# A fused pooled-attention, Fourier-mixing and two-layer channel block: the third batch's front end in the second block, later stages moved by one to three groups, and the residual in three tiles

## The chip, the cores and the metric

The kernel runs on one core of one Trainium2 chip. A core has five engines with queues of their own: TensorE (PE, and PEld for its weight loads), VectorE (DVE), ScalarE (ACT), GpSimd (POOL) and SyncE (SP, which issues most DMAs). The metric is the device time of one execution in microseconds; a lower time is better. A program is timed several times and the median counts; besides, one execution is recorded by the hardware profiler, and its trace is what is read here.

## The reference

Eight batches of eight heads, 576 tokens, 64 channels a head, go through an attention whose keys and values are means over eight neighbouring tokens (72 keys). The result, as 512 channels for each token, is mixed by a two-dimensional Fourier transform, normalised over the channels, and put through two layers with a relu between:

```
k_p = k.reshape(B, H, 72, 8, D).mean(axis=3)       # B, H, S, D = 8, 8, 576, 64
v_p = v.reshape(B, H, 72, 8, D).mean(axis=3)
attn = softmax(scale * q @ k_p^T)
x = (attn @ v_p) as [B, S, 512]
u = x + real(fft(fft(x, axis=1), axis=2))
un = (u - mean(u)) / sqrt(var(u) + 1e-6)           # over the 512 channels
out = u + relu(un @ w_ch1) @ w_ch2                 # 512 -> 2048 -> 512
```

All is float32. The matmuls of the two layers split each operand in a high part and a rest, and add three products (high x high, high x rest, rest x high).

## The kernel before

**Two streams of work.** The first is the *front end* of a batch, function `fe(b)` (L313): everything from the load of q and k to the normalised operands `unh{b}` and `unl{b}`. It is a generator of 31 steps; each `yield` ends one. The second is the *main loop*, `fast()` (L863) with `plain()` (L840) for its first block: the two layers over nine blocks of 512 tokens. As a batch has 576 tokens, block k takes the first tokens of batch k and what was left of batch k-1, so block k cannot begin before the front end of batch k has written its operands, and the second product group of a block reads the last of them.

**The front end's steps,** with the names used below (the digit behind a name is the batch): load of q and k, and the sums of eight keys on POOL (L344, tile `ks`); the scores `psS` on PE (L409), their maxima on DVE (L411, L414) and exponentials on ACT (L418); the transposes `psT`, `psV` and `psR` (L446, L456, L467); the products with v, `psX` (L489); a split of the result in a high part and a residue `f` (L573, L574); the first Fourier side `psA` (L613) and `psB` (L630); the second, `psQ` and `psP` (L647), whose sums go through DVE (L653 to L663) and POOL (L674 to L682) into `U` or `X`; the mean over channels `psM` (L719, L723); the centred tokens (L725); their squares `lf` on ACT and DVE (L734 to L740); the variance `psVar` on PE: L749 to L754 from batch 2 on, where ACT casts half of the squares (`qhl`, L749) and DVE the rest (L750), and L767 to L786 with diagonal tiles `dg` for batches 0 and 1; three Newton rounds on ACT and DVE for one over the root (L755 to L762); the scaling on POOL (L794); the operands (L701 to L705).

**The main loop's steps.** In block 0, `plain()` runs a group of twelve matmuls (tile `g`, L850) for each of 16 rows of channels, then the relu and its residue (L855, L856), and then `gemm2` (L814) adds the row's part of the second layer into `acc`, twelve matmuls in three pieces of four. From block 1 on, a step takes two rows of channels at once: seven product groups of six matmuls (`x`, L911), whose sums run through DVE (L870 and L915), and two relus (L878 to L880), with the pieces of the second layer of the step before ("g" in the lists `MID`, `FIRST`, `LAST`) between them. All PSUM banks but `acc`'s are shared from then on: products and front-end tiles take the next of four buffers of one tag in turn (`shared`, L293). At a block's end `evict` (L825) adds `acc` to the residual `U` and sends it out (L838).

**What sets the order.** The main loop counts its groups: `pos` in the listing. At each group `advance(pos)` (L965) takes a front-end step of batch c when `pos` has passed the entry of a table for that step plus the batch's start, `90 + 104 * (c - 2)`, or 0 for batch 1. So an entry is the number of groups from the start of the block ahead of the batch's own; a negative entry lies in the block before that. Batch 1 has the table `AT1`, batch 2 `AT2`, all others `AT` (L57 to L59). Up to group 92 (`MANUAL`) the order on PE is the scheduler's, which may move an instruction; behind it PE runs in program order. The order on the other engines is the scheduler's throughout. An engine runs its queue in order: what waits holds up all behind it.

**The residual and the staged weights.** `U` (L121) is one tile, `[128, 4, 1728]`, with three slots of 576 columns, and batch b lives in slot `b % 3` (`slot`, L75). Ahead of the main loop its first two slots hold q and k of batch 0, and the third takes pieces of the weights as they come from memory: `load_w` (L166) brings each piece to one of four places, two in that third slot and two in `sx`; `prep_w` (L184) then splits it with ACT, DVE and POOL operations (L194 to L208), `combine` (L223) makes sums of pieces (L235), and DMAs write them to scratch memory, from where `feed` (L258) brings them back block by block through a ring of twelve buffers.

Of the kernel before, what the change touches and what calls it, by code (L numbers as in the profile page):

```python
# [22 lines left out]
P = 128  # L23
# [51 lines left out]
def slot(b):  # L75
    return (b % 3) * S


def cuts(t0, t1, every):

    r = []
    while t0 < t1:
        e = min(t1, (t0 // every + 1) * every)
        r.append((t0, e))
        t0 = e
    return r

# [6 lines left out]
def tile_kernel(ctx: ExitStack, tc: tile.TileContext, qt, kt, vm, vr, w1, w2, cad, cbd, mkd, out):  # L94
    nc = tc.nc
    cp = ctx.enter_context(tc.tile_pool(name="cp", bufs=1))
# [34 lines left out]
    def flat(t):  # L131
        return t.rearrange("p c n -> p (c n)")
# [33 lines left out]
    def load_w(n):  # L166
# [928 lines left out]
```

## Time and profile before

| | |
|---|---|
| median of three runs | 1133.4 us (1131.36, 1133.4, 1134.22) |
| the profiled execution's own time | 1137.14 us |
| its span, first to last instruction | 1135.3 us |
| mean granted tensor clock over the span | 0.954 |
| end of block 0's stretch, first product of block 1 | 267.15 us |
| first products of blocks 2 to 6 | 386.15, 502.37, 617.39, 733.5, 850.4 us |
| memory traffic | 217.63 MB read, 30.67 MB written |

A row of the timeline has a start in microseconds, the duration, the engine, the line, the operation, `out<-in` by the program's names without their numbers, the tiles' sizes and the number of instructions taken together; in brackets stands how long the engine idled ahead of the row, and the instruction that ended the wait. A granted clock of 1.00 is full speed. The profiled execution is one execution of its own, a little longer than the median of the runs.

### The profile page before, as it was taken

What the parts mean: (1) busy time and instruction counts of PE and PEld (TensorE: products, weight loads), DVE (VectorE), ACT (ScalarE), POOL (GpSimd) and SP (SyncE); (2) the same over time, 40 slices, a digit from 0 to 9 for tenths busy, and PEclk for the clock granted to TensorE, in tenths of its full rate; (3) what the DMA queues carried; (4) which work ended last, traced back from release to release, by engine and by line L of the source; (5) the groups of instructions that cost most, each with busy time, mean ns of one, the idle gap of its engine ahead of it and who ended that gap; (6) DMA issues with size and microseconds to landing.
All of it is one profiled execution on the core that took longest, in us unless ns stands there. A gap on an engine that the chain in (4) does not pass through costs nothing.

```text
span 1135.3 us, 19340 instructions
## 1 busy us (share of the span) xinstructions
PE 1028.5 (91%) x6118; PEld 887.8 (78%) x6118; DVE 754.9 (66%) x1479; ACT 568.0 (50%) x1698; POOL 574.1 (51%) x531
## 2 busy tenths in 40 slices
PE   6778988767899899999999999999999999999998
PEld 4456666546788788888888888888888988988987
DVE  7579865877767775777578766876687567433333
ACT  6577754555435653576346734574367333322221
POOL 4357566663663656465645564556554244322221
PEclk8789988987999999999999999999999999999999
DMA  8628858454666676677766776777576667888884
GB/s 284 201 74 269 305 164 274 147 191 158 225 212 208 185 262 216 195 214 254 234 190 218 246 249 187 220 247 239 187 216 194 202 199 225 287 262 255 294 258 144
DMA packets 142756, 249.58 MB, mean 220 GB/s; under 512 B 15808, under 2 KB 36288, under 8 KB 142400
## 3 DMA queue, kind: packets, MB, share of 16 engines
q1 hardware_dynamic: 142368, 245.69, 67.7%
q0 software_dynamic: 288, 2.66, 0.6%
q8 instruction: 50, 0.82, 0.3%
q14 instruction: 50, 0.41, 0.1%
HBM read 217.63 MB, written 30.67 MB: 219 GB/s over the span
## 4 chain that ended last, share of the span: by engine, by line
PE 53%; DVE 17%; ACT 11%; DMA 7%; issue 5%; POOL 4%; SPq 0%; DVEq 0%; POOLq 0%; ACTq 0%
PE acc L814 24%; PE x L911 20%; ACT t L418 2%; PE psS L409 2%; DMA sx<-in_w 2%; DMA k<-in_kt 2%; PE psP L647 1%; PE psB L630 1%; DMA w1op<-w1s 1%; DMA out<-U 1%; DVE sx L870 1%; PE psX L489 1%; DVE lf L740 1%; DVE X L705 1%; PE psQ L647 1%
## 5 line engine op out<-in xcount | busy, mean ns | idle before, releaser
L911 PE MATMUL x<-unh,w1op 128*128 128x256 f32 x1792 | 345.4, 282 | 17.1 <-DVE R L475 3.7
L911 PEld LDWEIGHTS x<-unh,w1op 128*128 128x128 f32 x1792 | 289.3, 189 | 53.5 <-DVE sx L870 6.0
L870 DVE TENSOR_TENSOR sx<-x,sx 128x256 f32<-128x256 f32 (+1 forms) x384 | 176.1, 464 | 144.7 <-PE x L911 137.2
L880 POOL TENSOR_TENSOR hl<-sx,hh 128x512 fp32r<-128x512 f32 x128 | 171.3, 1338 | 199.7 <-ACT hh L879 179.8
L878 ACT ACTIVATE sx<-sx 128x512 f32<-128x512 f32 x128 | 80.9, 632 | 218.4 <-DVE sx L870 218.1
L911 PE MATMUL x<-unl,w1op 128*128 128x256 f32 x896 | 176.7, 279 | 0.0
L814 PE MATMUL acc<-hh,w2low 128*128 128x512 f32 x576 | 167.4, 405 | 0.0
L911 PEld LDWEIGHTS x<-unl,w1op 128*128 128x128 f32 x896 | 136.9, 189 | 0.0
L814 PEld LDWEIGHTS acc<-hh,w2low 128*128 128x128 f32 x576 | 102.1, 192 | 15.2
L814 PE MATMUL acc<-hh,w2high 128*128 128x512 f32 x324 | 94.1, 398 | 5.0 <-ACT hh L855 5.0
L418 ACT ACTIVATE t<-psS,mx 128x72 f32<-128x72 f32 x280 | 86.4, 345 | 21.0 <-DVE mx L414 12.5
L814 PE MATMUL acc<-hl,w2high 128*128 128x512 f32 x324 | 93.7, 397 | 0.0
L426 POOL TENSOR_TENSOR t<-t,sm 128x720 f32<-128x720 f32 x32 | 47.7, 1492 | 76.1 <-DVE sm L425 52.3
L879 ACT CAST hh<-sx 128x512 fp32r<-128x512 f32 x128 | 79.4, 620 | 3.7
L814 PE MATMUL acc<-hl,w2h 128*128 128x512 f32 x252 | 75.9, 425 | 1.5 <-DVE hl L856 1.5
L814 PE MATMUL acc<-hh,w2h 128*128 128x512 f32 x252 | 71.2, 406 | 4.0 <-ACT hh L855 4.0
L814 PEld LDWEIGHTS acc<-hh,w2high 128*128 128x128 f32 x324 | 56.4, 190 | 13.7 <-ACT hh L855 5.7
L409 PE MATMUL psS<-kpb,q 128*128 128x144 f32 x280 | 51.3, 336 | 14.6 <-DVE R L475 7.2
L418 ACT ACTIVATION_READ_ACCUMULATOR t<-psS,mx 128x1 f32 x280 | 64.4, 231 | 0.0
L814 PEld LDWEIGHTS acc<-hl,w2high 128*128 128x128 f32 x324 | 56.6, 189 | 8.5 <-issue 0.4
L409 PEld LDWEIGHTS psS<-kpb,q 128*128 128x128 f32 x280 | 46.6, 229 | 19.4 <-DVE R L475 7.8
L344 POOL TENSOR_TENSOR k<-k 128x288 f32<-128x288 f32 (+1 forms) x56 | 36.1, 645 | 48.9 <-DMA k<-in_kt 47.5
(267 smaller groups left out, 1959.3 us busy)
## 6 DMA issues: line engine op xcount, KB each, us to landing
w1op<-w1s SPq DMA_DIRECT2D x448, 256.0 KB, 3.4
w2low<-w2l SPq DMA_DIRECT2D x128, 256.0 KB, 3.4
w2high<-w2d SPq DMA_DIRECT2D x72, 256.0 KB, 3.7
U<-in_w SPq DMA_DIRECT2D x16, 512.0 KB, 4.5
sx<-in_w SPq DMA_DIRECT2D x16, 512.0 KB, 5.1
q<-in_qt SPq DMA_DIRECT2D x28, 288.0 KB, 3.0
k<-in_kt SPq DMA_DIRECT2D x28, 288.0 KB, 2.9
v<-in_vm SPq DMA_DIRECT2D x28, 256.0 KB, 2.8
```

Source lines behind the costliest of these rows:

```text
L344: nc.gpsimd.tensor_tensor(out=out if n == 1 else src[:, :, 0:n], in0=src[:, :, 0] if n == 1 else src[:, :, 0:n], in1=src[:, :, 1] if n == ...
L409: nc.tensor.matmul(ps[:, c * W2J:(c + 1) * W2J], lhsT=q[:, r0:r0 + P], rhs=kpb[g % 2], start=True, stop=True)
L418: nc.scalar.activation(t[:, c0 + c, h], pv[:, c, h], AF.Exp, scale=1.0 / 64.0, bias=mx[x], accum_out=sm[x])
L426: ins = nc.gpsimd.tensor_tensor(out=t, in0=t, in1=sm.unsqueeze(3).broadcast_to([P, 5, 2, J]), op=ALU.mult)
L489: behind["X", b] = nc.tensor.matmul(ps, lhsT=w, rhs=a, start=(i == 0), stop=(i == len(mm) - 1))
L647: nc.tensor.matmul(ps, lhsT=w, rhs=a, start=(i == 0), stop=(i == 6))
L814: nc.tensor.matmul(acc[e], lhsT=a[:, e], rhs=h, start=(f == 0 and x == 0), stop=(f == NFC - 1 and x == 2))
L870: nc.vector.tensor_tensor(out=o, in0=x, in1=y, op=ALU.add)
L878: nc.scalar.activation(c, c, AF.Relu)
L879: nc.scalar.copy(out=h, in_=c)
L880: nc.gpsimd.tensor_tensor(out=l, in0=c, in1=raw(h), op=ALU.subtract)
L911: nc.tensor.matmul(ps, lhsT=w[:, q, i], rhs=t[:, 2 * c + i], start=(n == 0), stop=(n == 5))
```

## The change

The table of batch 2 is rewritten: its first entry was -36, in block 0, and is now -6 with the next at 3, and its last ones before 104, from 76 to 79, are now 88 to 90. In the table of batches 3 to 7, `AT`, thirteen entries grow by one or two groups and two shrink by one; the variance's (index 25, `psVar`) goes from 76 to 78. The tile `U` becomes three tiles `Us[0]` to `Us[2]`, and the two places for staged weights in the third of them become contiguous pieces of 1024 columns. The functions `slot` and `cuts` (which nothing calls) go. The set of instructions is the same before and after.

```
@@ -26,7 +26,6 @@
-RING = 3 * S
@@ -54,8 +53,8 @@
 RES = [0, 2, 5, 7, 9, 12, 14]
 
 UNITS0, UNITS, MANUAL, TAIL = 90, 104, 92, (2, 8, 14, 20, 26)
-AT = [-36, -28, -23, -5, -3, -1, 2, 13, 14, 16, 18, 25, 27, 28, 38, 41, 44, 47, 51, 52, 55, 57, 60, 66, 66, 76, 76, 77, 78, 79, 104]
-AT2 = [-36, -28, -23, -13, -11, -9, -6] + AT[7:]
+AT = [-36, -28, -23, -5, -2, 0, 3, 13, 14, 16, 19, 25, 27, 28, 39, 42, 45, 48, 51, 52, 55, 57, 60, 65, 65, 78, 78, 79, 80, 81, 104]
+AT2 = [-6, 3, 7, 20, 23, 25, 28, 30, 32, 38, 41, 46, 48, 48, 58, 60, 63, 65, 67, 67, 70, 72, 74, 78, 78, 88, 88, 89, 89, 90, 104]
 AT1 = [-1] * 7 + [2 + 3.5 * n for n in range(17)] + [64, 69, 71, 73, 74, 75, 96]
 E0, O0, E1, O1 = 0, 1, 2, 3
 
@@ -70,20 +69,6 @@
-def slot(b):
-    return (b % 3) * S
...
@@ -118,7 +103,7 @@
     rw = [cp.tile([96, P], F32R, name=f"rw{i}") for i in range(2)]
     xe = cp.tile([P, 290], F32R, name="xe")
     X = cp.tile([P, 4, S], F32, name="X")
-    U = cp.tile([P, 4, RING], F32, name="U")
+    Us = [cp.tile([P, 4, S], F32, name=f"U{i}") for i in range(3)]
     rb = cp.tile([P, S + 1024], F32, name="rb")
     xt0 = rb[:, 2 * S:2 * S + 256].rearrange("p (c n) -> p c n", c=4)
     uns = {}
@@ -172,7 +157,7 @@
             return
         x = place[n]
         if x < 2:
-            st = U[:, 2 * x:2 * x + 2, 2 * S:2 * S + DM].bitcast(I32)
+            st = flat(Us[2])[:, 1024 * x:1024 * (x + 1)].bitcast(I32).rearrange("p (r x) -> p r x", r=2)
         else:
             st = sx[:, 1024 * (x - 2):1024 * (x - 1)].bitcast(I32).rearrange("p (r x) -> p r x", r=2)
         nc.sync.dma_start(st, src.bitcast(I32).rearrange("p (r x) -> p r x", r=2))
@@ -311,17 +296,16 @@
 
 
     def fe(b):
-        ro = slot(b)
-        Ub = U[:, :, ro:ro + S]
+        Ub = Us[b % 3]
         Xb = Ub if b else X
         st = {}
         halves = [slice(0, HS), slice(HS, S)]
 
         def load(g):
 
-            k = U[:, g, S:2 * S] if b == 0 else wk.tile([P, S], F32, tag="k", name=f"k{b}_{g}")
+            k = Us[1][:, g] if b == 0 else wk.tile([P, S], F32, tag="k", name=f"k{b}_{g}")
             nc.sync.dma_start(k, kt[b, g])
-            q = U[:, g, 0:S] if b == 0 else wk.tile([P, S], F32, tag="q", bufs=2, name=f"q{b}_{g}")
+            q = Us[0][:, g] if b == 0 else wk.tile([P, S], F32, tag="q", bufs=2, name=f"q{b}_{g}")
             nc.sync.dma_start(q, qt[b, g])
             st["q", g], st["k", g] = q, k.rearrange("p (j w) -> p j w", w=POOLW)
 
@@ -828,7 +812,7 @@
             for b, t0, n, col in segs:
                 if n == 0:
                     continue
-                y = slice(slot(b) + t0, slot(b) + t0 + 2 * n)
+                U, y = Us[b % 3], slice(t0, t0 + 2 * n)
                 a = acc[e].rearrange("p (h x) -> p h x", h=2)[:, :, col:col + n]
                 u = U[:, e, y].rearrange("p (h x) -> p h x", h=2)
                 if k == 0:
```

What the tables do to the queues is shown by the order of the instructions, before and after. A row is one instruction, or as many alike as the x at its end tells; the names carry numbers here, the first of which is the batch (`psS2_3_0` is a score tile of batch 2).

The first place is TensorE around the first product of block 1, `x<-unh1`. Before, the rows ahead of it are:

```order
L785 MATMUL psVar1_1968<-dg_2001,avg_75 128x288
L446 MATMUL psT2_2_2080<-ident_74,t2_2_1866 128x128 x4
L785 MATMUL psVar1_1968<-dg_2001,avg_75 128x288
L456 MATMUL psV2_0_2097<-ident_74,t2_3_1769 128x128
L456 MATMUL psV2_0_2097<-ident_74,t2_2_1866 128x128
L457 MATMUL psV2_0_2097<-ident_74,rt_1796 32x128
L467 MATMUL psR2_0_2105<-ident_74,rt_1796 32x128 x4
L409 MATMUL psS2_0_0_2128<-kpb0_76,q2_0_1919 128x144 x3
L409 MATMUL psS2_0_3_2140<-kpb0_76,q2_0_1919 128x144 x2
L409 MATMUL psS2_1_0_2175<-kpb1_77,q2_1_1929 128x144 x3
L409 MATMUL psS2_1_3_2187<-kpb1_77,q2_1_1929 128x144 x2
L911 MATMUL x_2251<-unh1_2017,w1op_2054 128x256 x2
```

After the change the same place reads:

```order
L631 MATMUL psP1_2_1616<-cb_72,A0_1287 128x290 x3
L631 MATMUL psP1_2_1616<-cb_72,A1_1288 128x290 x3
L631 MATMUL psP1_2_1616<-cb_72,AB2_1289 128x290
L703 MATMUL psM1_1704<-s_1656,avg_75 128x288
L703 MATMUL psM1_1707<-s_1656,avg_75 128x288
L751 MATMUL psVar1_1821<-avg_75,lf_1756 128x1 x5
L769 MATMUL psVar1_1821<-dg_1854,avg_75 128x288 x2
L895 MATMUL x_2033<-unh1_1870,w1op_1907 128x256 x2
L895 MATMUL x_2033<-unl1_1871,w1op_1907 128x256 x2
L895 MATMUL x_2033<-unh1_1870,w1op_1907 128x256 x2
L393 MATMUL psS2_3_0_2044<-kpb1_77,q2_3_1960 128x144 x3
L393 MATMUL psS2_3_3_2056<-kpb1_77,q2_3_1960 128x144 x2
```

Batch 2's scores and transposes have left the stretch between batch 1's last stages and block 1; its first scores stand behind block 1's first product group. From batch 1's `psB` to its `psVar` no row of another kind stands between.

The second place is TensorE in the last third of block 3, where batch 4's variance is computed. Before:

```order
L911 MATMUL x_6185<-unh3_3696,w1op_6084 128x256 x2
L911 MATMUL x_6185<-unl3_3697,w1op_6084 128x256 x2
L911 MATMUL x_6185<-unh3_3696,w1op_6084 128x256 x2
L753 MATMUL psVar4_6201<-qhl_6198,avg_75 128x288
L754 MATMUL psVar4_6201<-qhl_6198,avg_75 128x288
L753 MATMUL psVar4_6205<-qhl_6198,avg_75 128x288
L754 MATMUL psVar4_6205<-qhl_6198,avg_75 128x288
L409 MATMUL psS5_3_0_6217<-kpb1_77,q5_3_6108 128x144 x3
L409 MATMUL psS5_3_3_6229<-kpb1_77,q5_3_6108 128x144 x2
L814 MATMUL acc3_0_5335<-hl_6043,w2h_69 128x512
```

After:

```order
L393 MATMUL psS5_3_3_6215<-kpb1_77,q5_3_6110 128x144 x2
L798 MATMUL acc3_0_5337<-hl_6045,w2h_69 128x512
L798 MATMUL acc3_1_5338<-hl_6045,w2h_69 128x512
L798 MATMUL acc3_2_5339<-hl_6045,w2h_69 128x512
L798 MATMUL acc3_3_5340<-hl_6045,w2h_69 128x512
L895 MATMUL x_6260<-unh3_3669,w1op_6088 128x256 x2
L895 MATMUL x_6260<-unl3_3670,w1op_6088 128x256 x2
L895 MATMUL x_6260<-unh3_3669,w1op_6088 128x256 x2
L737 MATMUL psVar4_6271<-qhl_6268,avg_75 128x288
L738 MATMUL psVar4_6271<-qhl_6268,avg_75 128x288
L737 MATMUL psVar4_6275<-qhl_6268,avg_75 128x288
L738 MATMUL psVar4_6275<-qhl_6268,avg_75 128x288
```

The variance of batch 4 now stands behind batch 5's scores, a piece of the second layer and one more product group; before, it stood ahead of those scores.

The third place is POOL in block 0, at the residue `f` of batch 1 that `psB` reads. Before (`wdh` are sums of weights, `ks` sums of keys, `v2` and `k2` tiles of batch 2):

```order
L235 TENSOR_TENSOR wdh_86<-wdh_86,wdl_87 128x512
L344 TENSOR_TENSOR ks_1658<-k2_3_1650 128x72
L208 TENSOR_TENSOR w2low_1504<-wdl_87,w2high_1502 128x512
L235 TENSOR_TENSOR wdh_86<-wdh_86,wdl_87 128x512
L574 TENSOR_TENSOR f_1386<-tmpO_1255,f_1385 128x2x288
L344 TENSOR_TENSOR v2_1_2419<-v2_1_2419 128x64x4
L235 TENSOR_TENSOR wdh_86<-wdh_86,wdl_87 128x512 x2
L344 TENSOR_TENSOR v2_1_2419<-v2_1_2419 128x64x2
L344 TENSOR_TENSOR k2_2_1664<-k2_2_1664 128x72x4
```

After:

```order
L328 TENSOR_TENSOR k2_2_1972<-k2_2_1972 128x72x4
L328 TENSOR_TENSOR k2_2_1972<-k2_2_1972 128x72x2
L328 TENSOR_TENSOR ks_1976<-k2_2_1972 128x72
L328 TENSOR_TENSOR k2_0_2190<-k2_0_2190 128x72x4
L328 TENSOR_TENSOR k2_0_2190<-k2_0_2190 128x72x2
L328 TENSOR_TENSOR ks_2194<-k2_0_2190 128x72
L328 TENSOR_TENSOR k2_1_2200<-k2_1_2200 128x72x4
L558 TENSOR_TENSOR f_1388<-tmpO_1257,f_1387 128x2x288
```

The sums of weights are done ahead of this place now, and the key sums of three of batch 2's tiles, 2, 0 and the first step of 1, stand ahead of `f`; before, of the key tiles only 3 did.

More of the change, by code (lines that the diff above doesn't have):

```diff
@@ L28 @@
 NFC = FF // P
-RING = 3 * S
 BLK = 512
@@ L56 @@
 UNITS0, UNITS, MANUAL, TAIL = 90, 104, 92, (2, 8, 14, 20, 26)
-AT = [-36, -28, -23, -5, -3, -1, 2, 13, 14, 16, 18, 25, 27, 28, 38, 41, 44, 47, 51, 52, 55, 57, 60, 66, 66, 76, 76, 77, 78, 79, 104]
-AT2 = [-36, -28, -23, -13, -11, -9, -6] + AT[7:]
+AT = [-36, -28, -23, -5, -2, 0, 3, 13, 14, 16, 19, 25, 27, 28, 39, 42, 45, 48, 51, 52, 55, 57, 60, 65, 65, 78, 78, 79, 80, 81, 104]
+AT2 = [-6, 3, 7, 20, 23, 25, 28, 30, 32, 38, 41, 46, 48, 48, 58, 60, 63, 65, 67, 67, 70, 72, 74, 78, 78, 88, 88, 89, 89, 90, 104]
 AT1 = [-1] * 7 + [2 + 3.5 * n for n in range(17)] + [64, 69, 71, 73, 74, 75, 96]
@@ L72 @@
 REBIAS = 2.0 ** -112
[L75 to L86, printed above, removed]
 def raw(ap):
@@ L120, in tile_kernel @@
     X = cp.tile([P, 4, S], F32, name="X")
-    U = cp.tile([P, 4, RING], F32, name="U")
+    Us = [cp.tile([P, 4, S], F32, name=f"U{i}") for i in range(3)]
     rb = cp.tile([P, S + 1024], F32, name="rb")
@@ L174, in load_w @@
         if x < 2:
-            st = U[:, 2 * x:2 * x + 2, 2 * S:2 * S + DM].bitcast(I32)
+            st = flat(Us[2])[:, 1024 * x:1024 * (x + 1)].bitcast(I32).rearrange("p (r x) -> p r x", r=2)
         else:
@@ L313, in fe @@
     def fe(b):
-        ro = slot(b)
-        Ub = U[:, :, ro:ro + S]
+        Ub = Us[b % 3]
         Xb = Ub if b else X
@@ L320, in load @@
         def load(g):
-            k = U[:, g, S:2 * S] if b == 0 else wk.tile([P, S], F32, tag="k", name=f"k{b}_{g}")
+            k = Us[1][:, g] if b == 0 else wk.tile([P, S], F32, tag="k", name=f"k{b}_{g}")
             nc.sync.dma_start(k, kt[b, g])
-            q = U[:, g, 0:S] if b == 0 else wk.tile([P, S], F32, tag="q", bufs=2, name=f"q{b}_{g}")
+            q = Us[0][:, g] if b == 0 else wk.tile([P, S], F32, tag="q", bufs=2, name=f"q{b}_{g}")
             nc.sync.dma_start(q, qt[b, g])
@@ L830, in evict @@
                     continue
-                y = slice(slot(b) + t0, slot(b) + t0 + 2 * n)
+                U, y = Us[b % 3], slice(t0, t0 + 2 * n)
                 a = acc[e].rearrange("p (h x) -> p h x", h=2)[:, :, col:col + n]
```

## The prediction

> **What bounds the kernel now.** I read the page first: the share of each engine, and the tensor clock by slices.
>
> ```profile
> PE 1028.5 (91%) x6118; PEld 887.8 (78%) x6118; DVE 754.9 (66%) x1479; ACT 568.0 (50%) x1698; POOL 574.1 (51%) x531
> ...
> PEclk8789988987999999999999999999999999999999
> ```
>
> TensorE (PE) is the bound: it is busy 1028.5 of 1135.3 us, and no other engine passes 66%. The lost time lies at the front, where the clock row shows 7, 8 and 9. The view of stretches, cut at the start of each of the kernel's blocks, puts numbers on that (columns: stretch, its length, busy time with instructions of PE, weight loads, DVE, ACT, POOL, then granted clock, DMA share, GB/s).
>
> ```profile
> 83.00:267.15 184.15, 142.91 (x596) 108.06 (x595) 142.41 (x232) 111.10 (x322) 121.45 (x105) 0.87 0.67 215
> 267.15:386.15 119.00, 110.06 (x690) 98.05 (x691) 85.05 (x160) 56.82 (x167) 62.14 (x60) 0.96 0.66 211
> ...
> 617.39:733.50 116.11, 111.11 (x717) 98.78 (x716) 84.09 (x175) 63.97 (x212) 66.31 (x63) 0.99 0.71 224
> ```
>
> Block 0 (83 to 267) leaves PE idle 41 us at a clock of 0.87. Block 1 takes 119 us with 690 matmul records, a later block 116 with 717. So the change has three places: the end of block 0, block 1 with its passage to block 2, and five like passages later. The first product of block 1, from the timeline of PE (in brackets the idle time before a row and what ended it), waits for an exponential of the third batch:
>
> ```profile
> 267.15 0.79 PE L911 MATMUL x<-unh,w1op 128*128 128x256 f32 x2 [3.30 <-ACT t L418]
> ```
>
> **Part A, block 0.** The third batch's scores and transposes (35 matmuls, 40 exponentials) leave the stretch ahead of 267.15. But the order of the change also puts all sixteen first-layer groups ahead of batch 1's psB, psQ, psP, psM and psVar, which then follow each other with nothing between. So the start of block 1 is the time of the last group plus that chain. First the time of the last group. Its last residue on DVE ended at 242.0:
>
> ```profile
> 241.31 0.69 DVE L856 SCALAR_TENSOR_TENSOR hl<-g,hh 128x512 fp32r<-128x512 f32 x1
> ...
> 83.00:150.00 67.00, 59.22 (x254) 45.04 (x254) 55.18 (x82) 48.15 (x133) 46.61 (x39) 0.95 0.87 289
> 200.00:242.00 42.00, 32.21 (x142) 25.90 (x143) 34.10 (x57) 23.04 (x73) 28.72 (x27) 0.89 0.60 191
> sum 242.00, PE 189.04 PEld 141.47 DVE 177.74 ACT 148.80 POOL 146.54; mean PE 47.26 PEld 35.37 DVE 44.43 ACT 37.20 POOL 36.64
> ```
>
> DVE is the fullest engine beside PE. In the order 38 of its instructions leave the part ahead of that row (the maxima and residues of the third batch, the squares of the second) and 6 come; the mean of the stretch from 200 is 34.10 / 57 = 0.6 us, and at 0.47, since many of them are small reductions, 32 net are 15 us: 177.7 busy us become 162.7. By 150 us 112.2 of them are done; the other 50.5 take 62 us at the 81% of 200 to 242, which gives 212, and at the 73% of the whole stretch it would be 222. I take 217, and 218 for psB behind it. Now the chain, each step from rows:
>
> ```profile
> 57.17 2.96 PE L630 MATMUL psB<-ca,f 128*128 128x256 f32 x18
> 198.40 0.97 PE L647 MATMUL psQ<-cb,B 128*128 128x288 f32 x6
> 204.12 0.29 PE L647 MATMUL psP<-cb,AB 98*128 98x290 f32 x1
> 206.51 2.00 POOL L681 TENSOR_TENSOR U<-X,U 128x288 f32<-128x288 f32 x2
> 213.02 3.79 POOL L682 TENSOR_TENSOR U<-X,U 128x288 f32<-128x288 f32 x4
> 220.56 1.34 DVE L725 TENSOR_TENSOR X<-U,psM 128x1152 f32<-128x1152 f32 x1
> 578.58 0.69 ACT L734 ACTIVATE lf<-X 128x576 f32<-128x576 f32 x1 [3.72 <-DVE X L725]
> 583.02 1.73 DVE L740 TENSOR_TENSOR lf<-lf 128x576 f32<-128x576 f32 x1
> 236.48 2.27 PE L767 MATMUL psVar<-avg,lf 128*128 128x1 f32 x10 [2.72 <-DVE lf L740]
> 247.49 2.62 POOL L794 TENSOR_TENSOR X<-X,rb 128x1152 f32<-128x1152 f32 x1 [4.71 <-ACT rb L786]
> 260.28 1.41 DVE L702 TENSOR_TENSOR unl<-X,unh 128x896 fp32r<-128x896 f32 x2
> ```
>
> psB 3.0; psQ and psP 198.40 to 204.41, 6.0; from there to the centred X 2.1 until POOL starts, its six halves 2.00 + 3.79, and 1.34 on DVE, 9.3; squares 578.58 to 584.75, 6.2; psVar to the scaling 236.48 to 247.49, 11.0; scaling and operands 247.49 to 261.69, 14.2. The sum is 49.7; the last two held exponentials and transposes of batch 2, for which I take 3 off (nothing at the one end, 6 at the other): 47. So the second product group of block 1, which needs the last operands, runs at 218 + 47 = 265, against 267.15 + 0.7 = 267.85: **A = -3**. The gain of the emptier engines is nearly eaten by a chain that PE used to hide. The bounds need the pace of product groups where PE waits for nothing:
>
> ```profile
> 598.03 1.09 PE L814 MATMUL acc<-hh,w2high 128*128 128x512 f32 x4
> 598.96 0.40 PE L911 MATMUL x<-unh,w1op 128*128 128x256 f32 x2
> ...
> 599.67 0.62 PE L814 MATMUL acc<-hh,w2low 128*128 128x512 f32 x2
> ```
>
> Four matmuls of the second layer take 0.93 (598.03 to 598.96), a group of the first 0.71. In block 0 the products left from 83 on are 372 matmuls, 86.5 us, with 15 of batch 1: PE alone would be done at 184. psB as early as 200, halfway to that, makes A = -21; as late as 232 (second rival), A = +11.
>
> **Part B, block 1.** The 35 matmuls come back here:
>
> ```profile
> 388.56 1.39 PE L409 MATMUL psS<-kpb,q 128*128 128x144 f32 x10
> ...
> 379.22 0.61 PE L467 MATMUL psR<-ident,rt 128*32 128x128 f32 x4 [0.71 <-DVE sx L870]
> 381.65 0.50 PE L911 MATMUL x<-unh,w1op 128*128 128x256 f32 x2 [1.81 <-DVE al L451]
> ...
> 380.00:384.00 4.00, 2.35 (x11) 2.02 (x12) 3.85 (x8) 3.71 (x10) 2.52 (x3) 0.84 0.18 50
> 384.00:388.00 4.00, 4.00 (x25) 3.96 (x24) 3.20 (x11) 1.80 (x8) 1.37 (x2) 0.73 0.52 146
> ```
>
> At 0.14 us each, the mean of these ten, they are 4.9 us. The batch's exponentials lie beside products, since ACT is busy only 57 of 119 us there. What they don't hide is the end of the batch: psVar of batch 2 now stands 8 product groups (0.71 us) and 7 groups of the second layer (0.93) ahead of block 2, 14 us with its psT, where it stood 25 before. Behind psVar come:
>
> ```profile
> 586.74 0.82 DVE L755 TENSOR_SCALAR lf<-psVar 128x288 f32<-128x288 f32 x2 [0.49 <-PE psVar L754]
> 598.99 0.71 ACT L760 ACTIVATE nt<-lf 128x576 f32<-128x576 f32 x1
> ...
> 601.84 3.87 POOL L794 TENSOR_TENSOR X<-X,rb 128x1152 f32<-128x1152 f32 x1 [4.93 <-DVE sm L424]
> ```
>
> 1.6 for variance and first guess, three Newton rounds of 2.8 (598.99 to 601.84), 3.9 for the scaling, and 8 for the operands of the second group (an estimate: the 14.2 of Part A without its scaling of 2.6 and 3.6 of overlap with batch 2): 22 us against 14 and the 1.4 of block 2's first groups, a wait of 6.5 to 7. It stalls everything in PE's queue behind it, the second layer of block 1 too. Add 1.7 for the clock after such a wait (Part C), and take off 4.2 for the waits of 0.71 and 1.81 and the clock of 0.84 and 0.73 over 4 us each (0.16 x 4 + 0.27 x 4 = 1.7), which this one replaces. 4.9 + 6.75 + 1.7 - 4.2: **B = +9**, from +3 (exponentials out of the way, chain 17) to +18 (DVE and ACT as full as in block 0).
>
> **Part C, batches 3 to 7.** Their psVar moves behind the next batch's psS and one more group of each layer.
>
> ```profile
> PE psVar L753 <- ACT qhl L749: 9.5, 6, 1.6
> ...
> 585.51 0.40 PE L753 MATMUL psVar<-qhl,avg 128*128 128x288 f32 x1 [1.59 <-ACT qhl L749]
> 586.30 0.40 PE L754 MATMUL psVar<-qhl,avg 128*128 128x288 f32 x1 [0.39 <-DVE qhl L750]
> ...
> 585.50:590.20 4.70, 4.29 (x18) 3.71 (x19) 4.05 (x9) 2.56 (x8) 1.28 (x1) 0.72 0.33 88
> 590.20:594.90 4.70, 4.70 (x34) 4.52 (x33) 2.57 (x7) 3.05 (x17) 0.19 (x1) 0.92 0.45 142
> ...
> 588.30 0.96 DVE L411 TENSOR_REDUCE mx<-psS 128x6 f32<-128x432 f32 x2
> ...
> L418 ACT ACTIVATE t<-psS,mx x280: 300/336/438, 59.5 to 860.7; 128x72 f32<-128x72 f32 x140
> ```
>
> Six such waits (one a batch, 2 to 7) cost 1.98 us each, and the clock falls to 0.72 and 0.92 in the two stretches of 4.7 us behind, another 0.36 x 4.7 = 1.7. After the change PE comes to psVar 3.3 us later (0.71 + 2 x 0.93 + 0.7), later than the 1.98 it waited. On ACT the cast it waits for stays ahead of the moved exponentials. But psVar's second half takes a PSUM bank that a product group held, whose reader on DVE now stands behind the two maxima (0.96, the row on DVE): I take 0.9 us of new wait, too short for the clock. Five batches at 1.98 + 1.7 - 0.9 = 2.8: **C = -14**, bounds -18 (no new wait) and 0 (third rival).
>
> The clock term is where the Trainium skill speaks against me: in "TensorE: Matmul & The Clock Gate", Part 1, the clock falls only after at least one idle window of about 3.4 us. By that a wait of 1.98 has no clock term, C would be 5 x 1.1 = -5.6, and the sum near no change. The rows above disagree: 0.72 behind 1.98 us of waiting, so I keep the term and give the rule a small chance.
>
> **Part D, the three tiles.** The residual's slots keep their sizes, and the staged weights lie in one piece. No wait on those loads stands on the path at more than a microsecond after block 0; cost 0, from -2 to +1.
>
> **Sum.** -3 + 9 - 14 = -8. The profiled execution took 1137.1 us (a span of 1135.3 and what lies around it), 3.7 more than the median of the runs (1133.4), so 1129 on its scale is **1125** as a median.
>
> **Rivals.** *Faster: block 0 speeds up.* DVE kept 82% from 83 to 150, and fell off only when batch 1's and batch 2's stages ran together. If psB starts at 200, A is -21 and the time 1107. Against it: the chain's start also needs POOL. Chance 0.23.
>
> *Slower: POOL's key sums stand ahead of batch 1's chain.* In the new order the residue that psB needs (f, L574) is behind the sums of three of batch 2's key tiles, which share one buffer, so each load waits for the sum before:
>
> ```profile
> 203.98 0.80 POOL L344 TENSOR_TENSOR k<-k 128x288 f32<-128x288 f32 x1 [2.95 <-DMA k<-in_kt]
> ```
>
> A load and its sum take 2.95 + 1.6 (three steps, the first 0.80 and the others half of it each), three of them 13.7. If they begin only when the groups end, psB goes from 218 to 232, A to +11 and the time to 1139. It decides above a psB at about 230. Chance 0.17.
>
> *Slower: psVar's wait changes hands.* If its second bank is that of the new scores, it waits for their maximum (0.5) and six exponentials, which start 0.3 us apart at the least (the row of L418): about 2.1 us, as long as now, with the clock. C is 0, the sum +6, the time 1139. Chance 0.14.
>
> *The clock falls by its own phase, whatever psVar does* (the page's rule): C = -5.6, time 1134. Chance 0.03.
>
> **How the numbers follow.** The forecast itself has 0.43; with B's and C's bounds it reaches 1112 to 1134. About 0.3% (3.4 us) is what a measurement of this kernel can tell from no change. Faster by more: 0.23 and 0.35 of the forecast, 0.58. Slower: both slow rivals but a little, and the forecast with B at its worst, 0.27. Within: 0.15. The range holds all the cases' middles, from 1101 to 1142.
>
> **What would show it.** Right: PE with psB to psVar in one run and mostly idle some 30 us before block 1; block 1 longer by about 9 us with a wait at the second group of block 2; L753's waits on L749 down to one, and the clock at 1.00 in blocks 2 to 6, each near 113 us instead of 116. Wrong: psB before 205 or after 230, or clock dips that stay.

## The result, and the profile after

| | before | after |
|---|---|---|
| median of nine executions | 1132.26 us | 1139.33 us |
| ratio, 95% interval | 1 | 1.006 [1.0039, 1.0081] |
| the profiled execution's own time | 1137.14 us | 1135.42 us |

The change makes the kernel 0.6% slower. The forecast was 1125 us and faster. One of the nine executions of the kernel after took 3452.57 us and stands outside the ratio; the median of the other eight is 1138.86 us. The two profiled executions alone would mislead: that of before took longer than all nine timed ones (1129.7 to 1135.25 us) and that of after was the shortest of its nine, so the profiled executions differ by -2 us where the medians differ by +7. Stage lengths are therefore compared over several traces below, and totals by medians only.

The page of the kernel after, engine shares and granted clock by slices:

```profile
PE 1024.9 (90%) x6118; PEld 882.9 (78%) x6118; DVE 761.5 (67%) x1479; ACT 565.2 (50%) x1698; POOL 575.3 (51%) x531
...
PEclk8688999958999899999999999999999999999999
```

The shares tell nothing: they are those of before within one percentage point. The stretches do. For before, the three that the prediction didn't quote, the front up to the first product group of block 0, block 2, and blocks 3 to 6. The columns are those of the prediction's stretches, and a stretch can begin up to 0.6 us behind the first product of its block (block 7 of before begins at 959.13):

```profile
0.00:83.06 83.06, 56.82 (x239) 40.78 (x240) 57.06 (x110) 53.33 (x175) 37.30 (x57) 0.83 0.56 182
...
386.15:502.37 116.22, 110.82 (x715) 98.59 (x714) 83.38 (x173) 62.72 (x207) 64.73 (x62) 0.99 0.69 221
502.37:959.59 457.22, 436.92 (x2811) 389.66 (x2809) 321.21 (x670) 240.37 (x763) 240.34 (x215) 0.99 0.69 219
```

And for after, the same five stages, front, block 0, block 1, block 2, and blocks 3 to 6:

```profile
0.00:87.90 87.90, 56.22 (x218) 37.47 (x219) 75.31 (x124) 60.81 (x167) 50.95 (x62) 0.77 0.84 283
87.90:248.81 160.91, 129.36 (x561) 96.88 (x561) 110.86 (x179) 82.08 (x228) 97.99 (x92) 0.89 0.55 178
248.81:373.71 124.90, 115.85 (x735) 103.05 (x735) 89.23 (x189) 70.55 (x256) 68.32 (x64) 0.95 0.67 207
373.71:497.54 123.83, 113.24 (x712) 100.29 (x713) 90.61 (x181) 67.19 (x218) 70.11 (x66) 0.96 0.67 211
497.54:955.03 457.49, 436.81 (x2818) 389.69 (x2817) 329.69 (x673) 240.88 (x765) 239.97 (x215) 0.99 0.70 218
```

Stage by stage: the front is 4.8 us longer, block 0 is 23 shorter (184.09 to 160.91), block 1 is 5.9 longer, block 2 is 7.6 longer, blocks 3 to 6 are the same to 0.3 us, and what is left of the span behind them is 2.9 longer (178.6 against 175.7). So more than half of a large gain in block 0 is given back in the two blocks behind it, no gain shows where the variance was moved, and a loss stands in a stage that the prediction left out: the front, in which DVE is busy for 75 us instead of 57 and POOL for 51 instead of 37.

### The profile page after: what moved, and what is told of

Its sections match the earlier page's. It is cut to its first block, busy times and chain, and to the rows that moved or that the text cites. A ratio compares the mean times of both kernels' runs of the same rounds, so it can differ in the third digit from the quotient of the medians.

```text
span 1133.6 us, 19318 instructions
## 1 busy us (share of the span) xinstructions
PE 1024.9 (90%) x6118; PEld 882.9 (78%) x6118; DVE 761.5 (67%) x1479; ACT 565.2 (50%) x1698; POOL 575.3 (51%) x531
## 4 chain that ended last, share of the span: by engine, by line
PE 58%; DVE 19%; ACT 7%; POOL 6%; DMA 5%; issue 4%; SPq 1%; POOLq 0%; DVEq 0%; ACTq 0%
PE acc L798 25%; PE x L895 21%; PE psX L473 2%; ACT t L402 2%; POOL X L778 2%; PE psP L631 2%; DVE X L689 2%; DVE mx L395 1%; DMA k<-in_kt 1%; PE psB L614 1%; DVE unl L686 1%; DMA sx<-in_w 1%; PE g L834 1%; DVE sx L854 1%; PE psQ L631 1%
## 5 line engine op out<-in xcount | busy, mean ns | idle before, releaser
L895 PE MATMUL x<-unh,w1op 128*128 128x256 f32 x1792 | 350.4, 284 | 24.0 <-ACT unh L685 10.5
L895 PEld LDWEIGHTS x<-unh,w1op 128*128 128x128 f32 x1792 | 291.6, 190 | 62.5 <-ACT unh L685 12.3
L895 PE MATMUL x<-unl,w1op 128*128 128x256 f32 x896 | 178.5, 281 | 3.3 <-DVE unl L686 3.3
L798 PE MATMUL acc<-hh,w2low 128*128 128x512 f32 x576 | 164.4, 399 | 0.0
L895 PEld LDWEIGHTS x<-unl,w1op 128*128 128x128 f32 x896 | 137.4, 189 | 4.3 <-DVE unl L686 4.3
L798 PE MATMUL acc<-hl,w2high 128*128 128x512 f32 x324 | 96.6, 407 | 0.0
L798 PE MATMUL acc<-hl,w2h 128*128 128x512 f32 x252 | 70.3, 399 | 4.2 <-DVE hl L840 4.2
L686 POOL TENSOR_TENSOR unl<-X,unh 128x256 fp32r<-128x256 f32 (+11 forms) x28 | 38.0, 1368 | 43.7 <-ACT unh L685 42.9
L328 POOL TENSOR_TENSOR v<-v 128x256 f32<-128x256 f32 (+1 forms) x48 | 45.8, 953 | 19.9 <-DMA v<-in_vm 19.1
```

The lines of the kernel that those rows point to most:

```text
L328: nc.gpsimd.tensor_tensor(out=out if n == 1 else src[:, :, 0:n], in0=src[:, :, 0] if n == 1 else src[:, :, 0:n], in1=src[:, :, 1] if n == ...
L686: e.tensor_tensor(out=l, in0=x, in1=raw(h), op=ALU.subtract)
L798: nc.tensor.matmul(acc[e], lhsT=a[:, e], rhs=h, start=(f == 0 and x == 0), stop=(f == NFC - 1 and x == 2))
L895: nc.tensor.matmul(ps, lhsT=w[:, q, i], rhs=t[:, 2 * c + i], start=(n == 0), stop=(n == 5))
```

## The experiments

Time and ratio are against runs of the kernel before on the same chip (medians 1131.98 to 1132.17 us). First the change was taken apart: tiles alone, and tiles with one table each. The four kernels have the lines of the kernel after; tables are its own unless the diff says otherwise.

**e1_after_again: the change once more.** No edit.

> The changed kernel once more, for a second trace and more times. The trace at hand took 1135.4 us, the lowest of its runs, and the trace of before 1137.1, above its own median; so the two traces differ by -2 us where the medians differ by +7. Theory 1 (the loss is in the order, at the passage to block 2): median 1139 again, and the second trace again has block 1 near 125 us and block 2 near 124, with the part before block 1 longer by some 4 us than the 248.8 of the first trace. Rival (the loss is a part of the tail that varies): the part before block 1 stays near 249 and blocks 3 to 8 are longer by 4 us or more.

Measured: 1138.52 us, 1.005 [1.0029, 1.0071]. Its trace has the front at 90.1 us, block 0 at 162.3, block 1 at 126.9, block 2 at 123.0, blocks 3 to 6 at 456.7. Theory 1 was half right: the part before block 1 is 3.7 us longer than in the first trace and blocks 1 and 2 are long again; but the front is slow again too, and theory 1 has no place for that.

**e2_tiles_only: both tables as before.**

```
-AT = [-36, -28, -23, -5, -2, 0, 3, ... 78, 78, 79, 80, 81, 104]
-AT2 = [-6, 3, 7, 20, 23, 25, 28, ... 88, 88, 89, 89, 90, 104]
+AT = [-36, -28, -23, -5, -3, -1, 2, ... 76, 76, 77, 78, 79, 104]
+AT2 = [-36, -28, -23, -13, -11, -9, -6] + AT[7:]
```

> Both tables as before; of the change only the three tiles and the staged weights in contiguous pieces stay. Theory 1 (the tables cost, the tiles nothing): 1132, the time of before, within 2 us. Rival (the tiles move the loads and the dependences of the front, whose first product group came 4.8 us later in the changed kernel's trace): 1136 or more, with the first group of block 0 near 88 us instead of 83.

Measured: 1138.86 us, 1.0049 [1.0029, 1.0068]: the whole loss, without either table. Its first two stages:

```profile
0.00:87.94 87.94, 56.79 (x219) 38.93 (x219) 74.68 (x124) 60.95 (x167) 51.41 (x62) 0.83 0.84 282
87.94:272.38 184.44, 146.00 (x615) 109.83 (x615) 132.28 (x219) 102.33 (x329) 107.78 (x100) 0.85 0.51 162
```

The front is as long as after the change, with the same busy DVE; block 0 is as long as before. My theory 1 fell, and its rival, written beside it, held. The cost lies in the part that I had priced at nothing.

**e3_tiles_and_batch2_table: the later table as before.**

```
-AT = [-36, -28, -23, -5, -2, 0, 3, ... 78, 78, 79, 80, 81, 104]
+AT = [-36, -28, -23, -5, -3, -1, 2, ... 76, 76, 77, 78, 79, 104]
```

> Three tiles and the new table of batch 2; the table of batches 3 to 7 as before. Theory 1 (batch 2's table makes the loss, the shift of the variance in batches 3 to 7 brings nothing, since its wait only changes hands): 1139, the time of the changed kernel, within 2 us, and blocks 3 to 6 as long as before, 115 to 117 us each. Rival (the shift brings what I forecast, 14 us, hidden behind a larger loss of batch 2's table): 1150 or more.

Measured: 1139.71 us, 1.0055 [1.003, 1.008]. Within 1.2 us of e1 and e2: in the total, batch 2's table is worth nothing either way on top of the tiles, and the forecast gain of the later table isn't there.

**e4_tiles_and_later_table: batch 2's table as before.**

```
-AT2 = [-6, 3, 7, 20, 23, 25, 28, ... 88, 88, 89, 89, 90, 104]
+AT2 = [-36, -28, -23, -13, -11, -9, -6, 13, 14, 16, 18, ... 76, 76, 77, 78, 79, 104]
```

> Three tiles and the new table of batches 3 to 7; batch 2's table as before. Theory 1: 1132 within 2 us, as e2_tiles_only; the wait of the variance matmul on the cast of the squares is gone and one of about 1.2 us on the copy of a product sum stands in its place. Rival (the shift gains): 1118 to 1126. Third (the shift itself loses, by waits that the products now meet): 1135 or more.

Measured: 1142.44 us, 1.0081 [1.005, 1.0112]. The median is 3.6 us above e2's, so the new later table seems to cost time on its own (the intervals overlap); the third case of the expectation is nearest, and the gain is excluded.

**What the tiles do.** The front of the kernel after shows it. On PE, the first product group of block 0 waits for batch 0's operands:

```profile
87.90 3.78 PE L834 MATMUL g<-unh 128*128 128x512 f32 x8 [6.35 <-ACT unh L674]
```

These come late, because weights are worked on ahead of them. The first piece staged in the third tile is taken up at 15 us, on ACT:

```profile
15.10 0.77 ACT L181 ACTIVATE wdh<-U 128x512 uint16<-128x512 uint8 x1
```

and its later operations meet batch 0 on DVE and POOL. From the timeline of DVE of the kernel after, a step of batch 0's softmax, ten columns wide:

```profile
28.25 4.82 DVE L408 TENSOR_SCALAR sm<-sm 128x10 f32<-128x10 f32 x1
```

and from that of POOL, the first and last of the four weight residues beside it:

```profile
28.07 1.29 POOL L193 TENSOR_TENSOR w1low<-wdh,unh 128x512 fp32r<-128x512 f32 x1
...
31.78 1.25 POOL L193 TENSOR_TENSOR w2low<-wdl,w2high 128x512 fp32r<-128x512 f32 x1
```

In the kernel before, the same softmax step takes 0.15 us, and the two pieces staged in the residual's third slot are taken up only at 73 to 80 us. Its rows, on DVE:

```profile
27.14 0.15 DVE L424 TENSOR_SCALAR sm<-sm 128x10 f32<-128x10 f32 x1
...
79.68 0.45 DVE L198 TENSOR_SCALAR wdh<-U 128x512 uint16<-128x512 uint16 x1
```

and on ACT:

```profile
73.10 0.79 ACT L196 ACTIVATE wdl<-U 128x512 uint16<-128x512 uint8 x1 [0.91 <-POOL U L682]
```

That last row is the key: the preparation of a weight in the third slot waits for batch 0's residual, written to the first slot (L682). The two don't share a byte, but they share a tile; with three tiles the wait is gone and the same work starts at 15 us. The shared tile put the weights behind batch 0's front end, by chance at the right place; three tiles take that away, and the scheduler brings the weights' work to the head of the queues, in front of the batch that all wait for. It shows on SP as well: between 24 and 50 us the trace of after issues 17 transfers of weights, that of before five, and batch 1's first keys are asked for at 53.70 us instead of 47.16. The next four kernels test that.

**e5_tables_one_tile: the tables without the tiles.** The kernel before with both new tables:

```
-AT = [-36, -28, -23, -5, -3, -1, 2, ... 76, 76, 77, 78, 79, 104]
-AT2 = [-36, -28, -23, -13, -11, -9, -6] + AT[7:]
+AT = [-36, -28, -23, -5, -2, 0, 3, ... 78, 78, 79, 80, 81, 104]
+AT2 = [-6, 3, 7, 20, 23, 25, 28, ... 88, 88, 89, 89, 90, 104]
```

> The residual in one tile as before, both new tables. Theory (the tiles alone cost the 6.6 us that e2_tiles_only lost, and the tables' gain in block 0 and their loss in blocks 1 and 2 cancel): 1132 within 2 us, first product group of block 0 at 83 us, block 0 near 162 us long, blocks 1 and 2 together 15 to 17 us longer than before. Rival (the shorter block 0 was possible only because the tiles let the weights be prepared early): block 0 stays near 175 us or more, and the time is 1140 or more.

Measured: 1134.68 us, 1.0025 [1.0008, 1.0042]; first group at 83.6 us, block 0 165.9 long, blocks 1 and 2 together 249.0 against 235.2 before. The front is back, as the theory says. The rest of the theory holds less well: the total is 0.7 us outside its 2 us, blocks 1 and 2 lose 13.8 and not 15 to 17, and block 0 is 4 to 7 us longer than with tiles and the same table (158.9 to 162.3). Why block 0 is longer was not followed up.

**e6_tiles_strided: the layout of the staged pieces.** On e2:

```
-            st = flat(Us[2])[:, 1024 * x:1024 * (x + 1)].bitcast(I32).rearrange("p (r x) -> p r x", r=2)
+            st = Us[2][:, 2 * x:2 * x + 2, 0:DM].bitcast(I32)
```

> Tables as before and three tiles, but the staged weights in the third tile with the layout of before: two rows of 512 columns, 576 apart, in place of one piece of 1024. Theory (what costs is that the weights' preparation is no longer held behind batch 0's residual, whatever the layout): as e2_tiles_only, 1139 within 2 us, first group at 88 us or later. Rival (the contiguous pieces change the transfers, and these cost): 1132, first group at 83 us.

Measured: 1136.16 us, 1.0039 [1.0017, 1.0061]; first group at 88.8 us. The front's loss stays with the old layout, so the layout is not its cause. The time is 0.8 us outside the theory's 2 us, and 2.7 below e2's with intervals that overlap: whether the layout adds something elsewhere stays open.

**e7_tiles_held: the tiles, with the order restored.** On e2 (the operations of `prep_w` queued behind instructions of batch 0's front end on their own engines; no wait is added):

```
+                behind["C", 0] = nc.scalar.copy(out=xh[:, ti, x:y], in_=X[:, ti, x:y])
+                ins = engine(ti, UL).tensor_tensor(out=xl[:, ti, x:y], ...)
+                if ti == 0:
+                    behind["D", 0] = ins
...
+            with tc.issue_after(behind["C", 0].ins) if n < 2 else ...:
                 nc.scalar.activation(hi.bitcast(F32), hi.bitcast(F32), AF.Copy, scale=REBIAS)
+            with tc.issue_after(behind["B", 0].ins) if n in (0, 1, 4) else ExitStack():
                 nc.scalar.activation(dh[:, :, :, 0], ...)
+            with tc.issue_after(behind["D", 0].ins) if n < 2 else ExitStack():
                 nc.vector.tensor_scalar(out=dh[:, :, :, 1], ...)
```

> As e2_tiles_only, but the first two staged weight pieces of the third tile are queued on ACT and DVE behind batch 0's sums and centred operands, where they stood before. Theory: first group of block 0 back at 83 us and the time at 1132 to 1134. Rival (the loss lies behind the first group, in transfers or waits of block 0): 1138 or more with the first group at 83 us.

Measured: 1130.8 us, 0.999 [0.9966, 1.0014], 1.2 below the theory's range. The loss is gone. Front, block 0, block 1 and block 2 of its trace (in this kernel and the later ones on e8, L899 is the L895 of the kernel after):

```profile
0.00:82.97 82.97, 52.75 (x240) 37.20 (x240) 56.98 (x110) 52.65 (x175) 37.40 (x57) 0.86 0.56 183
82.97:263.16 180.19, 144.26 (x596) 109.00 (x595) 147.32 (x232) 110.38 (x322) 123.22 (x105) 0.82 0.67 220
263.16:380.42 117.26, 109.14 (x690) 97.24 (x691) 84.08 (x160) 56.69 (x166) 61.69 (x60) 0.97 0.68 214
380.42:497.51 117.09, 110.70 (x715) 99.09 (x714) 84.25 (x173) 62.82 (x207) 64.31 (x62) 0.98 0.69 220
```

The front is 83.0 us with DVE at 57, as before. Same tiles, same work, another order of it: the order is what the tiles cost. Of the 8.1 us between the medians of e2 and e7, the two traces put 5.0 in the front and 4.2 in block 0 (184.4 and 180.2).

**e8_change_held: the whole change with the hold.** The edit of e7 on the kernel after.

> The whole change with the same hold as e7_tiles_held. Theory: what e1_after_again takes less the 5 to 7 us of the front, 1132 to 1134, and equal to e5_tables_one_tile. Rival (the late preparation takes the gain of block 0 away): block 0 longer than 170 us, time 1139 or more.

Measured: 1131.1 us, 0.9996 [0.9979, 1.0013], 7.4 below e1. That it should equal e5 didn't hold: it is 3.6 us below it. The same stages:

```profile
0.00:83.97 83.97, 57.71 (x239) 41.42 (x240) 57.74 (x110) 53.39 (x175) 37.51 (x57) 0.90 0.55 181
83.97:243.28 159.31, 127.29 (x541) 95.37 (x540) 127.56 (x192) 90.44 (x221) 113.30 (x97) 0.89 0.73 241
243.28:369.37 126.09, 114.38 (x735) 102.12 (x736) 91.91 (x189) 70.82 (x256) 67.30 (x64) 0.97 0.67 205
369.37:492.64 123.27, 112.86 (x716) 99.79 (x717) 90.58 (x181) 66.69 (x217) 69.71 (x65) 0.97 0.68 212
```

Against e7 this is the two tables alone: block 0 -20.9, block 1 +8.8, block 2 +5.6 (block 3 begins at 492.07 here and at 497.51 in e7), and from there to the end of the span +4.5 (636.8 against 632.3). With 1.0 in the front the trace is 1.0 shorter; the medians are 1131.1 against 1130.8.

**Where block 2 loses.** Its first products in the trace of e8, on PE:

```profile
373.33 0.76 PE L395 MATMUL psS<-kpb,q 128*128 128x144 f32 x4 [1.28 <-DVE sx L903]
377.77 0.80 PE L899 MATMUL x<-unh,w1op 128*128 128x256 f32 x2 [3.68 <-ACT unh L689]
379.67 0.80 PE L899 MATMUL x<-unl,w1op 128*128 128x256 f32 x2 [1.10 <-DVE unl L690]
```

Batch 2's operands are late, as the prediction has it. If that is all, its last stages have to stand earlier.

**e9_tail_earlier: batch 2's table closed up.** On e8:

```
-AT2 = [-6, 3, 7, 20, 23, 25, 28, 30, 32, 38, 41, 46, 48, 48, 58, 60, 63, 65, 67, 67, 70, 72, 74, 78, 78, 88, 88, 89, 89, 90, 104]
+AT2 = [-6, 1, 4, 15, 18, 20, 23, 25, 27, 32, 35, 39, 41, 42, 51, 53, 56, 58, 60, 60, 63, 65, 67, 71, 71, 80, 80, 81, 81, 82, 104]
```

> As e8_change_held, with batch 2's table closed up: the same first entry, its scores and products 2 to 5 groups earlier, its mean 7 and its variance 8 groups earlier (80 to 82 in place of 88 to 90). Theory (the 6 us by which block 2 is longer than with the old table are the wait for batch 2's operands at its start): block 2 back near 117 us, block 1 not longer than 127, time 1125 to 1127. Rival (block 1 has no room, its longer time is the same work met by full DVE and ACT): block 1 takes what block 2 gives, time 1130 to 1133.

Measured: 1126.23 us, 0.9949 [0.9931, 0.9967]: faster than both kernels. Its blocks 0, 1 and 2:

```profile
84.12:245.03 160.91, 128.52 (x552) 97.07 (x551) 132.04 (x198) 93.38 (x241) 112.34 (x98) 0.90 0.74 240
245.03:374.39 129.36, 115.57 (x725) 102.89 (x726) 95.14 (x187) 71.78 (x243) 71.47 (x67) 0.94 0.63 199
374.39:489.12 114.73, 109.92 (x713) 97.70 (x711) 85.60 (x176) 62.38 (x208) 65.14 (x62) 0.99 0.73 226
```

Counted from first product to first product, block 2 gives back 8.0 us and block 1 takes 3.3 of them. The net is near the 4.9 us of the medians, but the two traces also differ elsewhere (block 0 +1.6, from block 3 on -3.2), so the agreement is only rough. The theory's time holds; its bound for block 1 (127) was 2 us too low.

**e10_tail_earlier_old_later_table: e9 with the later table of before.** The edit of e3 on e9.

> As e9_tail_earlier with the table of batches 3 to 7 as before. Theory (the shift in that table is worth nothing): within 2 us of e9_tail_earlier. Rival (the shift loses, since the products meet other waits): 3 to 4 us less than e9_tail_earlier. Forecast of the prediction: 14 us more.

Measured: 1124.83 us, 0.9943 [0.9922, 0.9965], the fastest kernel here, though not apart from e9.

**e11_held_old_later_table: e8 with the later table of before.** The edit of e3 on e8.

> As e8_change_held with the table of batches 3 to 7 as before. Theory (the shift is worth nothing): 1131 within 2 us, the tensor engine waiting 8 us for the variance's casts in batches 3 to 7 where e8_change_held waits 4 for copies of sums and as much again elsewhere. Rival (the shift loses): 1127 to 1128. Forecast of the prediction: 1145.

Measured: 1130.03 us, 0.9984 [0.9963, 1.0004], 1.1 below e8. In both pairs (e8 and e11, e9 and e10) the shift of the later table is worth nothing that can be told in the total. The traces say more. Four pairs of kernels differ in that table alone; each cell has the old table, then the new one, in us, counted from the first products of blocks 1 and 3:

| pair | blocks 1 and 2 | block 3 to the end | median |
|---|---|---|---|
| e2, e4: batch 2's table of before | 232.6, 232.3 | 633.2, 637.5 | 1138.86, 1142.44 |
| e3, e1: batch 2's new table | 255.0, 249.9 | 631.9, 635.3 | 1139.71, 1138.52 |
| e11, e8: the same, held | 253.9, 248.8 | 632.5, 636.8 | 1130.03, 1131.1 |
| e10, e9: closed up, held | 248.3, 244.1 | 632.4, 633.6 | 1124.83, 1126.23 |

From block 3 on all seven traces with the old table take 629.1 to 633.2 us and all seven with the new one 633.6 to 637.5. So the shift loses 1 to 4 us where it was to win 14. Where batch 2's table is new, it also gives 4 to 5 us back in blocks 1 and 2, which hides the loss in the total; why it does was not followed up. As the expectation has it, the wait changes: behind 497 us TensorE waits 7.9 us for the variance's casts in e11, and in e8 3.8 us for copies of sums, 2.9 for `al` at the transposes `psV` and 3.0 for exponentials.

**e12_start_earlier: batch 2 begins in block 0.** On e9:

```
-AT2 = [-6, 1, 4, 15, 18, 20, 23, ... 71, 71, 80, 80, 81, 81, 82, 104]
+AT2 = [-14, -8, -2, 10, 13, 16, 19, 22, 25, 30, 33, 37, 39, 40, 49, 51, 54, 56, 58, 58, 61, 63, 65, 70, 70, 80, 80, 81, 81, 82, 104]
```

> As e9_tail_earlier with all of batch 2's front end another 8 groups earlier at the start (first entry -14, scores from -8 to 10) and 2 in the middle; the end at 80 to 82. Its scores of two head pairs then stand ahead of block 1's first product on TensorE. Theory (what the change wins in block 0 it wins because no exponentials of batch 2 stand ahead of batch 1's operands): block 0 longer than e9_tail_earlier's by 4 us or more and the time no better. Rival (there is room for them beside the chain): block 0 as in e9_tail_earlier and block 1 shorter, time 2 us or more below it.

Measured: 1130.46 us, 0.9975 [0.9955, 0.9995]. Its block 0:

```profile
82.98:249.84 166.86, 133.84 (x562) 102.58 (x561) 135.27 (x205) 98.00 (x265) 116.07 (x100) 0.85 0.71 234
```

Two head pairs' scores ahead of block 1's first product make block 0 6 us longer than in e9 (160.91). The first product waits 6.8 us for an exponential of batch 2, and the second product group comes to its `unl` at 256.27 instead of 252.80. The total is 4 us longer. The theory's numbers held.

## Why the prediction was wrong

**Part D is the first step that failed.** The prediction gave the three tiles 0 (from -2 to +1), since "no wait on those loads stands on the path at more than a microsecond after block 0". They cost 6.7 us by the medians of e2 and its runs of before, 5.5 by the ratio. I looked for a wait that the tiles would remove behind block 0, and not at what the wait did in the front: it held work back that competes with the path. The row on ACT at 73.10, waiting for `U` of L682, was in the trace of before and shows two parts of one tile that share nothing. With the hold the tiles cost nothing (e7) and the sum of the rest can be judged alone.

That rest is e8 against e7, and it gained nothing where the forecast had -8. Part C's -14 is missing, which is the largest error of the sum, and Part A gained some 13 more than its -3. That two errors of this size largely cancel is luck. What is left of them is the other half of the miss: without Part D's error the time would have been e8's 1131, not 1125.

**Part A, -3, was mis-sized: -16,** inside its bounds. The prediction counts it at the second product group of block 1: 264.61 in e7, 249.25 in e8 with a front 1.0 us longer. (Block 0 itself, up to the first group, is 20.9 shorter; the second group then waits for its operands.) The forecast put the groups' end at 217, `psB` behind it, to 221, and a chain of 44 behind that. The last residue of a group ended at 211.01 in the trace of after, with the front 4.8 us late, and at 209.28 in e8. There `psB` stands among the last groups and ended at 206.47, and the chain from there took 42.8 us; after, `psB` ended at 216.60 and the chain took 38.2. So the forecast had the start of the chain too late, by some 15 us against e8 and 9 against after, and the chain too long, by 1 and 6. DVE's load was right (167 us by the last residue of e8, against 163); but from 150 us on PE was busy 57.7 of the 59.3 us to that residue at a clock of 1.00, so the groups ran at PE's pace.

I compared 265 with the 267.85 of before, without seeing what that makes of before: there `psB` ended at 198.6, so before took 69 us from there to 267.85, for steps that add up to 46.7 without `psB`. The difference is waits, and other work, between the steps. The row of before, on PE:

```profile
197.70 0.87 PE L630 MATMUL psB<-ca,f 128*32 128x256 f32 x6
```

and of after:

```profile
214.06 1.45 PE L614 MATMUL psB<-ca,f 128*128 128x256 f32 x10 [1.48 <-POOL f L558]
215.71 0.89 PE L614 MATMUL psB<-ca,f 128*32 128x256 f32 x6 [0.21 <-DVE B L582]
...
254.78 0.80 PE L895 MATMUL x<-unh,w1op 128*128 128x256 f32 x2 [1.23 <-ACT unh L685]
```

`psB` does end later after the change, at 216.6 with the front 4.8 us late, but the second product group of block 1 comes at 254.78, 38 us behind it. The later `psB` comes with the tiles and not with the tables: it ended at 199.0 in e5, the tables without the tiles, and at 205.6 in e7, the tiles without the tables. What the chain loses with batch 2's new table are batch 2's exponentials and scores, which stood in the queues between its steps. From PE's timeline of e7, with the old table:

```profile
204.71 0.87 PE L616 MATMUL psB<-ca,f 128*32 128x256 f32 x6
...
252.70 2.77 PE L395 MATMUL psS<-kpb,q 128*128 128x144 f32 x10 [4.56 <-ACT t L404]
263.16 0.79 PE L899 MATMUL x<-unh,w1op 128*128 128x256 f32 x2 [7.70 <-ACT t L404]
```

and of e8, with the new one:

```profile
205.60 0.87 PE L616 MATMUL psB<-ca,f 128*32 128x256 f32 x6
...
236.64 1.33 PE L773 MATMUL psVar<-dg,avg 128*128 128x288 f32 x2 [0.49 <-ACT rb L774]
243.28 0.80 PE L899 MATMUL x<-unh,w1op 128*128 128x256 f32 x2 [5.32 <-ACT unh L689]
...
249.25 0.50 PE L899 MATMUL x<-unh,w1op 128*128 128x256 f32 x2 [1.41 <-ACT unh L689]
```

In e7 the first product waits 7.7 us for an exponential of batch 2, behind scores that wait themselves; in e8 it waits for its own operand. From the end of `psB` to the second group e7 takes 59.0 us and e8 42.8; e11, which differs from e7 in batch 2's table alone, takes 42.4. So batch 2's work in the queues cost 16 us, and e12 shows it from the other side. The "3 off" that I had for it was taken from a sum of steps that held few of these waits.

**Part B, +9, measured +12** (from the second product group of block 1 to that of block 2: 117.0 us in e7, 128.5 in e8), inside its +3 to +18. The mechanism was right: the second group of block 2 waits 3.68 and 1.10 us for batch 2's operands, where 6.75 were forecast, and e9 takes the end of batch 2 8 groups forward and gets 5 us back. The rest stays in block 1, whose TensorE is busy 5 us more (114.4 against 109.1). With the later table of before, as in e11, it would be +13.

**Part C, -14, measured a loss** (the table under e11: from block 3 on 1 to 4 us more; blocks 3 to 6 457.22 and 457.49 us). The step that failed is "0.9 us of new wait" as all that comes in place of the old one. The third rival, with a C of 0, was nearest; but the bank is not that of the new scores, and that its 1139 is the time measured is luck, since Part D's loss made it. The wait of the variance does change hands, to the bank of a product whose copy DVE has yet to make, at 1.25 us; and another wait, on a transpose of the next batch, grows to 1.56. After, PE of block 3:

```profile
586.21 0.40 PE L737 MATMUL psVar<-qhl,avg 128*128 128x288 f32 x1 [1.25 <-DVE sx L899]
...
610.46 0.69 PE L440 MATMUL psV<-ident,t 128*128 128x128 f32 x2 [1.56 <-DVE al L435]
```

and the clock of the stretches around them:

```profile
586.20:590.90 4.70, 4.69 (x32) 4.38 (x33) 3.50 (x8) 3.86 (x22) 1.31 (x1) 1.00 0.43 134
...
609.40:614.10 4.70, 3.64 (x14) 2.87 (x15) 4.38 (x8) 4.66 (x11) 3.98 (x3) 0.64 0.30 101
```

The clock stays at 1.00 behind the variance, as I forecast, and falls to 0.64 at the transpose. Wait and clock are met again at another step, and PE's idle time in blocks 3 to 6 is 20.3 us before (457.22 less 436.92 busy) and 20.7 after. Part of the loss lies in block 6, 107.5 to 109.2 us in the seven traces with the old table and 110.0 to 111.1 in those with the new one; where the rest arises stays open.

**The other rivals.** The key sums of POOL ahead of `f` cost the 1.48 us of the row above, not 13.7: POOL did wait 1.70, 3.06 and 2.95 us for the loads of such keys (at 202.50, 207.28 and 211.96), but most of it beside the last product groups. The faster block 0 came to its size, -21 to the first product, but its `psB` "at 200" ended at 206.47 in e8 and 216.60 after, and the rest is the emptier queue. The range held the time, for a reason that none of its cases had. Two slips of the sums changed nothing: 73% of DVE gives 219, not 222, and the forecast case with B at 3 and C at -18 gives 1115, not 1112.

## What to carry to other kernels

A tile is also an order: a buffer shared by unrelated data makes waits, and a scheduler's queue may owe its good order to one of them. Before splitting it, list what the shared tile holds back, and put that order into the code if it's wanted; here a few lines of queueing were worth the whole loss. When a chain is summed from its steps, sum the one of before in the same way and compare it with what the trace shows from its first row to its last: the difference is the waits that a change may remove, or move.

## What the runs showed of the hardware

A ten-column DVE operation that takes 0.15 us in the kernel before took 4.82 in the kernel after, from 28.25 to 33.07, and ended as the last of four POOL operations did (31.78 + 1.25). e2 has the same row at 4.83. In the trace of after, 26 of the 32 rows of this step have no POOL work beside them and took 0.11 to 0.17 us; the six that have took 0.17 to 4.82. The Trainium skill, "SBUF — State Buffer", section "Who interferes with whom", says that DVE in its two-port modes and GpSimd take a shared pair of ports for a whole instruction, and the other blocks fully. The rows agree in that the DVE row ends with POOL's work, but whether it was in such a mode no trace shows, and no run here took POOL's work away alone, so the cause of this stall is argued and not shown. Its 4.7 us are nearly the 4.8 that the front lost; that they are the same was not tested either.

The clock fell to 0.64 over 4.7 us in which PE was idle for 1.06 us, the end of a wait of 1.56, and stayed at 1.00 behind one of 1.25. The Trainium skill, "TensorE: Matmul & The Clock Gate", Part 1, lets it fall after at least one idle window of some 3.4 us; no such stretch of full idleness stands there, so if the window is read as full idleness, the measurement here differs from the page.
